# A chunk's scan in whole-chunk instructions, a shorter scale, and counting by a scan and two products

## The chip, the cores and the metric

The kernel runs on one core of one Trainium2 chip. The metric is the device time of one execution in microseconds (us); less is better. A core has TensorE (matrix products), VectorE, ScalarE and GpSimd (elementwise work), and queues of DMA transfers, of which SP's and GpSimd's matter here. Each engine executes its own instructions in their order; semaphores make one engine wait for another or for a transfer.

## The reference

There are 20224 tokens (4 sequences of 5056) with 256 channels each. First, along each sequence and for each channel, a gated recurrence:

```python
sig = 1.0 / (1.0 + np.exp(-f_logit))
f = lower_bound + (1.0 - lower_bound) * sig
for t in range(S):
    h = f[:, t] * h + (1.0 - f[:, t]) * x[:, t]
    y[:, t] = h
```

Then a mixture of eight experts, one for each token:

```python
logits = y @ w_gate                       # 8 columns
e_idx = argmax(logits, axis=1)
gate_w = softmax(logits)[e_idx]
eom = sigmoid(y @ w_output_gate)[e_idx]   # 8 columns
out = gate_w * eom * (relu(y @ w1[e_idx]) @ w2[e_idx])   # 256 -> 1024 -> 256
```

All products are made from pairs of 16-bit numbers, a high part and the low rest (high x high, high x low, low x high), after scaling by powers of two.

## The kernel before

**Chunks.** The inputs lie with channels on the 128 partitions, so a chunk of 512 tokens is two blocks (k = 0, 1) of 128 x 512. There are 40 chunks, the last of 256 tokens. `chunk` (L254) is a generator. A bare `yield` ends a round; `yield SMALL` or `yield BIG` stands ahead of one VectorE instruction. In its rounds a chunk does, in this order: tanh on ScalarE (L265); on VectorE (f - 1) * x, with f still the tanh (L269); on ScalarE the affine map from tanh to the gate f (L274); the recurrence by one scan instruction for each block, cut where a sequence ends (L280); the sum of squares of h on ScalarE (L287) and on TensorE (L291), from which `pow2` (L134) makes a power of two and its inverse in five steps on VectorE. As tanh stands in for the sigmoid, the scan's result still lacks a factor for each channel, `na`; it enters through `na2` at L291 and through `sa` (L296). Then the high half (L310, ScalarE) and the low half (L314, VectorE) of the scaled h, four DMA transposes on SP's queue that bring them into rows, one for each token (L307), and the products with the gates' weights (L329, 16 small matmuls). The result is brought back (L341) with the scale `li`.

**Routing.** Some fifteen small VectorE instructions find each token's expert (`oh`, a one for its expert, L372) and its factor. `before` (L383) counts: a product with a triangle of ones gives how many earlier tokens of a block went to the same expert, and a product with ones for each further block adds the earlier blocks; that is nb + 1 = 5 products for the four blocks of 128 tokens. With the running count `cnt` this gives each token a row `dst` in the scratch `scr` in DRAM, sorted by expert, and GpSimd's queue scatters the rows there (L433).

**Experts.** The weights of all eight experts are prepared once: 16 halves are loaded, normed (`prep_norm`, and `pow2` in `prep_scale`), and split into high (L614, ScalarE) and low (L619, VectorE). Meanwhile `early` (L831) computes two rounds of eight first tiles of 128 tokens, one for each expert: `gather` (L624) brings the tokens' rows from `scr` by a transposing DMA into `xq` and their factors into `mt`, both issued on SP's queue; `first1` makes the first product on TensorE in two halves (h = 0, 1), ScalarE brings it out (L719), `first_low` (L722) makes its low half on VectorE, `first2` the second product. `factors` (L644) multiplies the tokens' factors in `mt` by the expert's, into `fac`, which `evacuate` (L739) uses. From about 184 us on, `experts` (L921) does tiles of 256 tokens: a copy of the expert's first weights (L657, VectorE), `gemm1` (L669 to L671), `gemm2` (L702 to L704).

**Order.** `pump` (L790) takes every live chunk and the tile's tasks one round further; a new chunk begins every 8 rounds, and `load_chunk` for the next one is issued at a chunk's fifth round. Inside a round `together` (L153) puts small instructions of one chunk between those of others. Up to the cut at L907 a planner of the framework is free to reorder the instructions of VectorE, ScalarE, TensorE and GpSimd by its own simulated times; SP's queue and all that stands behind the cut keep the written order (`ordered`, L911). Behind the cut the small matmuls of a chunk are put one by one between an expert's triples of large ones (`aside`, `beside`, L227 and L232).

Of the kernel before, what the change touches and what calls it, by code (L numbers as in the profile page):

```python
# [24 lines left out]
EXPO = 0x7F800000  # L25
TW = 7
TX = 8
# [23 lines left out]
def tile_scan_moe(  # L51
# [66 lines left out]
    cinv = cp.tile([P, E], F32, name="cinv")  # L118

# [6 lines left out]
    na = cp.tile([P, KD], F32, name="na")  # L126
    na2 = cp.tile([P, KD, P], BF16, name="na2")
# [6 lines left out]
    def pow2(ss, t, nm):  # L134
# [5 lines left out]
        iv = sp.tile([P, w], F32, tag=nm + "i", name=nm + "i", bufs=3)  # L140
        yield SMALL
# [4 lines left out]
        nc.vector.tensor_scalar(vi, vi, EXPO, None, ALU.bitwise_and)  # L146
        yield SMALL
        nc.vector.tensor_scalar(sc, v, 2.0 ** (62 + t), None, ALU.mult)
        yield SMALL
        nc.vector.tensor_scalar(iv.bitcast(I32), sc.bitcast(I32), EXPO, None, ALU.bitwise_xor)  # L150
        return sc, iv
# [25 lines left out]
    gsq = cp.tile([P, KD * G], F32, name="gsq")  # L177
# [8 lines left out]
    gi4 = cp.tile([P, 1], F32, name="gi4")  # L186
    nc.vector.tensor_scalar(gi4, giv, 0.25, None, ALU.mult)
# [66 lines left out]
    def chunk(c):  # L254
# [5 lines left out]
        hss = sp.tile([P, KD], BF16, tag="hss", name="hss")  # L260
        cuts = [0] + [q for q in range(1, n) if (t0 + q) % S == 0] + [n]
        f = [ft[:, k, 0:n] for k in range(KD)]
        h = [xt[:, k, 0:n] for k in range(KD)]
        for k in range(KD):
            nc.scalar.activation(f[k], f[k], AF.Tanh, scale=0.5)  # L265
# [19 lines left out]
        with nc.allow_low_precision("a scale's bound"):  # L285
            for k in range(KD):
                nc.scalar.activation(f[k], h[k], AF.Square, accum_out=hss[:, k : k + 1])  # L287
# [6 lines left out]
        sa = sp.tile([P, KD], F32, tag="sa", name="sa")  # L294
        yield SMALL
        nc.vector.tensor_scalar(sa, na, sx, None, ALU.mult)  # L296
        li = sp.tile([P, 1], F32, tag="li", name="li")
        yield SMALL
        nc.vector.tensor_tensor(out=li, in0=ix, in1=gi4, op=ALU.mult)  # L299
# [8 lines left out]

        for k in range(KD):
            nc.scalar.activation(hl[:, 0, k, 0:n], xt[:, k, 0:n], AF.Copy, scale=sa[:, k : k + 1])  # L310
        yield
        for k in range(KD):
            yield BIG
            nc.vector.scalar_tensor_tensor(  # L314
                out=hl[:, 1, k, 0:n], in0=xt[:, k, 0:n], scalar=sa[:, k : k + 1], in1=hl[:, 0, k, 0:n],
                op0=ALU.mult, op1=ALU.subtract,
            )
            turn(0, k)
# [22 lines left out]
        nc.scalar.activation(lgp[:, 0:nb], pr[:, 0:nb], AF.Copy, scale=li)  # L341
# [28 lines left out]
        oh = small("oh", E, BF16)  # L370
# [10 lines left out]
        pk = pp.tile([P, (NB + 1) * E], F32, tag="rw", name="pk")  # L381
        ohf = oh[:, 0:nb].rearrange("p b e -> p (b e)")
        w = nb * E  # L383
        def before(s):
            ww = w if s == 0 else (nb + 1 - s) * E
            nc.tensor.matmul(
                out=pk[:, s * E : s * E + ww], lhsT=ones if s else tri, rhs=ohf[:, 0:ww], start=(s == 0), stop=(s == nb),
                skip_group_check=True,
            )
# [11 lines left out]
        pos = small("pos", E)  # L401
        yield SMALL
        nc.vector.tensor_tensor(
            out=pos[:, 0:nb], in0=pk[:, 0:w].rearrange("p (b e) -> p b e", e=E),
            in1=cnt.unsqueeze(1).to_broadcast([P, nb, E]), op=ALU.add,
        )
        cn = sp.tile([P, E], F32, tag="cnt", name="cnt", bufs=4)
# [599 lines left out]
```

## Time and profile before

| what | value |
|---|---|
| time, median of 3 runs (lowest, highest) | 989.14 us (987.89, 991.45) |
| the profiled execution: its time, its span | 990.77 us, 989.1 us |
| mean granted TensorE clock | 0.988 |
| busy: TensorE matmul, weight load | 907.7 us (92%), 819.7 us (83%) |
| busy: VectorE, ScalarE, GpSimd | 801.0 us (81%), 519.7 us (53%), 390.1 us (39%) |
| instructions of VectorE, ScalarE | 2639, 1075 |
| moved by DMA | 146.56 MB |

The span runs from the first to the last instruction. In a row of the profile L12 is line 12 of the kernel; `out<-in` names the tiles an instruction writes and reads; `x40` is how many there are. A group's row gives busy time and mean duration in ns, then the engine's idle time just ahead of those instructions and what ended it. Weight loads run beside matmuls, and matmuls overlap, so that their durations add up to more than the time they take. A wait is put down to what ended last.

### The profile page before, as it was taken

How to read it: one execution, taken by the hardware profiler on the slowest of the kernel's cores; microseconds unless marked ns; L12 is line 12 of the kernel's file. 1: busy time of each engine (PE TensorE's matmuls, PEld its weight loads, DVE VectorE, ACT ScalarE, POOL GpSimd, SP SyncE). 2: the span in 40 equal slices, each digit the busy share in tenths (PEclk: the TensorE clock that was granted, in tenths of full speed). 3: DMA queues.
4: the chain of work that ended last, by engine and by line, in shares of the span. 5: the costliest groups of instructions: out<-in, count | busy, mean ns of one | idle time of the engine just before them, and what ended most of it. 6: DMA issues, size and time to landing. Idle time of an engine off the chain costs nothing. (4 is left out here: it accounts for less than half of the span.)

```text
span 989.1 us, 30907 instructions
## 1 busy us (share of the span) xinstructions
PE 907.7 (92%) x9775; PEld 819.7 (83%) x9775; DVE 801.0 (81%) x2639; ACT 519.7 (53%) x1075; POOL 390.1 (39%) x378
## 2 busy tenths in 40 slices
PE   2258898899999999999999999999999999999993
PEld 2247887788888888888888888888888888899992
DVE  7989897888989988888898888888888886545550
ACT  6667675555555555555565555555555543333331
POOL 1432334434445454454545434455444443211111
PEclk9999999999999999999999999999999999999997
DMA  8899984855575657556576665655666544312120
GB/s 310 206 275 293 237 230 126 188 157 151 131 157 144 151 153 167 141 133 152 150 153 150 169 138 140 153 148 157 150 163 134 129 100 90 100 45 43 41 57 17
DMA packets 238558, 146.56 MB, mean 148 GB/s; under 512 B 202557, under 2 KB 204223, under 8 KB 238400
## 3 DMA queue, kind: packets, MB, share of 16 engines
q1 hardware_dynamic: 222752, 101.74, 44.9%
q0 software_dynamic: 15360, 42.74, 14.4%
q8 instruction: 95, 1.56, 0.7%
q14 instruction: 63, 0.52, 0.2%
q10 hardware_dynamic: 288, 0.02, 0.0%
HBM read 58.38 MB, written 44.49 MB: 104 GB/s over the span
## 5 line engine op out<-in xcount | busy, mean ns | idle before, releaser
L674 ACT ACTIVATE hh<-ph 128x512 f16<-128x512 f32 (+1 forms) x328 | 180.4, 550 | 307.8 <-PE ph L671 297.4
L669 PE MATMUL ph<-xq,w 128*128 128x256 f16 (+1 forms) x1312 | 330.4, 260 | 2.9 <-DMA xq<-scr 2.4
L671 PE MATMUL ph<-xq,w 128*128 128x256 f16 (+1 forms) x1312 | 331.1, 261 | 0.0
L670 PE MATMUL ph<-xq,w 128*128 128x256 f16 (+1 forms) x1312 | 330.9, 261 | 0.0
L750 POOL DMA_INDIRECT out_dram<-yo,mt x146 | 175.3, 1201 | 363.2 <-ACT yo L746 339.9
L704 PE MATMUL py<-w2s,hl 128*128 x1168 | 318.5, 273 | 0.0
L703 PE MATMUL py<-w2s,hh 128*128 x1168 | 318.4, 273 | 0.0
L702 PE MATMUL py<-w2s,hh 128*128 x1168 | 318.1, 272 | 0.0
L682 DVE SCALAR_TENSOR_TENSOR hl<-ph,hh 128x512 f16<-128x512 f32 (+1 forms) x328 | 204.9, 625 | 58.2 <-ACT hh L674 55.8
L433 POOL DMA_INDIRECT scr<-rows,dst x154 | 175.7, 1141 | 122.6 <-issue 109.3
L657 DVE COPY w<-w1s 128x2048 f16 x164 | 120.3, 734 | 35.1 <-PE ph L671 33.3
L669 PEld LDWEIGHTS <-w 128*128 128x128 f16 x1312 | 127.9, 98 | 14.3 <-DVE fac L649 2.7
L671 PEld LDWEIGHTS <-w 128*128 128x128 f16 x1312 | 128.0, 98 | 11.9
L670 PEld LDWEIGHTS <-w 128*128 128x128 f16 x1312 | 127.9, 97 | 9.7
L704 PEld LDWEIGHTS <-hl 128*128 128x128 f16 x1168 | 114.1, 98 | 13.8
L702 PEld LDWEIGHTS <-hh 128*128 128x128 f16 x1168 | 114.0, 98 | 11.4
L703 PEld LDWEIGHTS <-hh 128*128 128x128 f16 x1168 | 113.9, 98 | 10.6
L280 DVE TENSOR_TENSOR_SCAN xt<-ft,xt 128x512 f32<-128x512 f32 (+4 forms) x78 | 90.8, 1172 | 0.0
L746 ACT ACTIVATE yo<-py,fac 128x256 f32<-128x256 f32 x146 | 61.8, 468 | 26.7 <-PE py L704 26.1
L314 DVE SCALAR_TENSOR_TENSOR ft<-xt,sa,ft 128x512 f16<-128x512 f32 (+1 forms) x76 | 56.2, 744 | 20.1 <-ACT ft L265 18.3
L329 PEld LDWEIGHTS <-ft 128*128 128x128 f16 x600 | 51.7, 99 | 15.1 <-ACT ft L310 4.9
L310 ACT ACTIVATE ft<-xt,sa 128x512 f16<-128x512 f32 (+1 forms) x76 | 50.2, 707 | 23.3 <-DVE li L299 16.0
(171 smaller groups left out, 1298.7 us busy)
## 6 DMA issues: line engine op xcount, KB each, us to landing
ft<-in_fT_dram SPq DMA_DIRECT2D x37, 512.0 KB
xt<-in_xT_dram SPq DMA_DIRECT2D x37, 512.0 KB
w<-in_wT_dram SPq DMA_DIRECT2D x32, 512.0 KB
scr<-rows,dst POOLq DMA_INDIRECT x154
rows<-ft SPq DMA_TRANSPOSE x152
out_dram<-yo,mt POOLq DMA_INDIRECT x146
xq<-scr SPq DMA_TRANSPOSE x99
scr<-padt SPq DMA_DIRECT2D x9, 136.0 KB
```

The source lines that it names most:

```text
L280: nc.vector.tensor_tensor_scan(out=xt[:, k, a:z], data0=ft[:, k, a:z], data1=xt[:, k, a:z], initial=init, op0=ALU.mult, op1=ALU.add)
L433: ins = nc.gpsimd.indirect_dma_start(out=scr[:, :], out_offset=IOA(ap=dst[:, b : b + 1], axis=0), in_=rows[:, b, :], in_offset=None)
L657: nc.vector.tensor_copy(out=w, in_=w1f[:, ds(T["ev"] * (2 * WH) + h * 2 * QH, 2 * QH)])
L669: nc.tensor.matmul(out=o, lhsT=w[:, f, k, 0, :], rhs=T["xh"][:, k, 0:n], start=first, stop=False)
L670: nc.tensor.matmul(out=o, lhsT=w[:, f, k, 0, :], rhs=T["xl"][:, k, 0:n], start=False, stop=False)
L671: nc.tensor.matmul(out=o, lhsT=w[:, f, k, 1, :], rhs=T["xh"][:, k, 0:n], start=False, stop=last)
L674: nc.scalar.activation(hh[:, :, 0:n], ph[:, :, 0:n], AF.Relu)
L682: nc.vector.scalar_tensor_tensor(out=hl[:, :, 0:n], in0=ph[:, :, 0:n], scalar=0.0, in1=hh[:, :, 0:n], op0=ALU.max, op1=ALU.subtract)
L702: nc.tensor.matmul(out=o, lhsT=hh[:, i, c], rhs=wh, start=first, stop=False, skip_group_check=True)
L703: nc.tensor.matmul(out=o, lhsT=hh[:, i, c], rhs=wl, start=False, stop=False, skip_group_check=True)
L704: nc.tensor.matmul(out=o, lhsT=hl[:, i, c], rhs=wh, start=False, stop=last, skip_group_check=True)
L750: ins = nc.gpsimd.indirect_dma_start(out=out[:, :], out_offset=IOA(ap=T["mt"][:, b, 2:4].bitcast(I32), axis=0), in_=T["yo"][:, b, :], in_o ...
```

## The change

- Tanh is one instruction for the whole chunk (two blocks), then come the two affine maps, and the product on VectorE uses the finished gate: (f - 1) * x. The scan so gives -h in full, and the factors `na`, `na2` and `sa` go; the power of two is made negative instead.
- The squares, the high half and the low half are one instruction each for the whole chunk; the sum of squares has one column and one product with ones.
- `pow2` has four steps in place of five, for chunks and for weights.
- `li` goes: the gates' results are brought back with the chunk's inverse alone, and the gates' own scale `gi4` enters as the scale of the two exponentials.
- The ones of the experts go into one of two fixed tiles with a column of zeros ahead of the blocks (`ones_of`). A scan of 40 elements on VectorE (`upto`), which begins anew at each expert, sums the earlier blocks; one product with ones and one with the triangle then give all counts, the total in a fifth column, and the running count is added in one instruction instead of two.
- `factors` of a first tile is done with its second half's low part, not with the first's.
- Small tiles are set once at the start (`going`, `ones_of`: four memsets on GpSimd).

```diff
+    going = cp.tile([P, E * (NB + 1)], BF16, name="going")
+    nc.gpsimd.memset(going, 1.0)
+    nc.gpsimd.memset(going.rearrange("p (e b) -> p e b", e=E)[:, :, 0:1], 0.0)
+    ones_of = [cp.tile([P, E, NB + 1], BF16, name=f"onesof{i}") for i in range(2)]
+    for t in ones_of:
+        nc.gpsimd.memset(t, 0.0)
-    nc.vector.tensor_scalar(na, lbt, 0.5, -0.5, ALU.mult, ALU.add)
-    for k in range(KD):
-        nc.vector.tensor_scalar(na2[:, k, :], ones, na[:, k : k + 1], na[:, k : k + 1], ALU.mult, ALU.mult)
...
-        nc.vector.tensor_scalar(vi, vi, EXPO, 1, ALU.bitwise_xor, ALU.logical_shift_right)
-        nc.vector.tensor_scalar(vi, vi, EXPO, None, ALU.bitwise_and)
-        nc.vector.tensor_scalar(sc, v, 2.0 ** (62 + t), None, ALU.mult)
-        nc.vector.tensor_scalar(iv.bitcast(I32), sc.bitcast(I32), EXPO, None, ALU.bitwise_xor)
+        nc.vector.tensor_scalar(vi, vi, EVEN, 1, ALU.bitwise_and, ALU.logical_shift_right)
+        nc.vector.tensor_scalar(sc.bitcast(I32), vi, -1.0, float(top - (1 << 31 if minus else 0)), ALU.mult, ALU.add)
+        nc.vector.tensor_scalar(iv.bitcast(I32), vi, float(EXPO - top), None, ALU.add)
...
+        nc.scalar.activation(fb2, fb2, AF.Tanh, scale=0.5)
+        yield
         for k in range(KD):
-            nc.scalar.activation(f[k], f[k], AF.Tanh, scale=0.5)
-        yield
+            nc.scalar.activation(f[k], f[k], AF.Identity, scale=fa[:, k : k + 1], bias=fb[:, k : k + 1])
+        yield
         for k in range(KD):
             yield BIG
             nc.vector.scalar_tensor_tensor(
-                out=h[k], in0=f[k], scalar=1.0, in1=h[k], op0=ALU.subtract, op1=ALU.mult
+                out=xt[:, k, 0:n], in0=f[k], scalar=1.0, in1=xt[:, k, 0:n], op0=ALU.subtract, op1=ALU.mult
             )
-        yield
-        for k in range(KD):
-            nc.scalar.activation(f[k], f[k], AF.Identity, scale=fa[:, k : k + 1], bias=fb[:, k : k + 1])
...
-            for k in range(KD):
-                nc.scalar.activation(f[k], h[k], AF.Square, accum_out=hss[:, k : k + 1])
+            nc.scalar.activation(fb2, hb2, AF.Square, accum_out=hss)
-        for k in range(KD):
-            nc.tensor.matmul(out=pv, lhsT=na2[:, k, :], rhs=hss[:, k : k + 1], start=(k == 0), stop=(k == KD - 1))
-        yield
-        sx, ix = yield from pow2(pv, TX, "x")
-        nc.vector.tensor_scalar(sa, na, sx, None, ALU.mult)
-        nc.vector.tensor_tensor(out=li, in0=ix, in1=gi4, op=ALU.mult)
+        nc.tensor.matmul(out=pv, lhsT=ones, rhs=hss, start=True, stop=True)
+        yield
+        sx, ix = yield from pow2(pv, TX, "x", minus=True)
...
+        nc.scalar.activation(hl[:, 0, :, 0:n], hb2, AF.Copy, scale=sx)
+        yield
+        yield BIG
+        nc.vector.scalar_tensor_tensor(
+            out=hl[:, 1, :, 0:n], in0=hb2, scalar=sx, in1=hl[:, 0, :, 0:n], op0=ALU.mult, op1=ALU.subtract
+        )
...
+        upto = sp.tile([P, E * (NB + 1)], BF16, tag="upto", name="upto")
+        yield SMALL
+        nc.vector.tensor_tensor_scan(
+            out=upto, data0=going, data1=ohz.rearrange("p e b -> p (e b)"), initial=0.0, op0=ALU.mult, op1=ALU.add
+        )
...
-            ww = w if s == 0 else (nb + 1 - s) * E
-            nc.tensor.matmul(
-                out=pk[:, s * E : s * E + ww], lhsT=ones if s else tri, rhs=ohf[:, 0:ww], start=(s == 0), stop=(s == nb),
-                skip_group_check=True,
-            )
-        for s in range(nb + 1):
+            if s == 0:
+                o = pk.rearrange("p e b -> p (e b)")
+                nc.tensor.matmul(out=o, lhsT=ones, rhs=upto, start=True, stop=False, skip_group_check=True)
+            else:
+                nc.tensor.matmul(
+                    out=pk[:, :, 0:NB], lhsT=tri, rhs=ohz[:, :, 1:], start=False, stop=True, skip_group_check=True
+                )
+        for s in range(2):
             aside(before, s)
...
-        nc.scalar.activation(ex[:, 0:nb], dl[:, 0:nb], AF.Exp)
+        nc.scalar.activation(ex[:, 0:nb], dl[:, 0:nb], AF.Exp, scale=gi4[:, 0:1])
-        nc.scalar.activation(eg[:, 0:nb], gs[:, 0:nb], AF.Exp, scale=-1.0)
+        nc.scalar.activation(eg[:, 0:nb], gs[:, 0:nb], AF.Exp, scale=gi4[:, 1:2])
...
         for T, h in wait:
             tasks.append(first_low(T, h))
-            if h == 0:
+            if h == 1:
                 tasks.append(factors(T))
```

More of the change, by code (lines that the diff above doesn't have):

```diff
@@ L25 @@
 EXPO = 0x7F800000
+EVEN = 0x7F000000
 TW = 7
@@ L125, in tile_scan_moe, with pow2 @@
     fb = cp.tile([P, KD], F32, name="fb")
-    na = cp.tile([P, KD], F32, name="na")
-    na2 = cp.tile([P, KD, P], BF16, name="na2")
     nc.vector.tensor_scalar(fa, lbt, -0.5, 0.5, ALU.mult, ALU.add)
     nc.vector.tensor_scalar(fb, lbt, 0.5, 0.5, ALU.mult, ALU.add)
-    nc.vector.tensor_scalar(na, lbt, 0.5, -0.5, ALU.mult, ALU.add)
-    for k in range(KD):
-        nc.vector.tensor_scalar(na2[:, k, :], ones, na[:, k : k + 1], na[:, k : k + 1], ALU.mult, ALU.mult)
-    def pow2(ss, t, nm):
+    def pow2(ss, t, nm, minus=False):
         w = ss.shape[1]
@@ L140, in pow2 @@
         iv = sp.tile([P, w], F32, tag=nm + "i", name=nm + "i", bufs=3)
+        top = EVEN // 2 + ((62 + t) << 23)
         yield SMALL
@@ L174, in alone @@
                 return end.value
-    gsq = cp.tile([P, KD * G], F32, name="gsq")
+    gsq = sp.tile([P, NB, 2 * G], F32, tag="lgp", name="gsq").rearrange("p b g -> p (b g)")[:, 0 : KD * G]
     gss = cp.tile([P, 1], BF16, name="gss")
@@ L185, in tile_scan_moe @@
     gsc, giv = alone(pow2(pgs, TW, "gt"))
-    gi4 = cp.tile([P, 1], F32, name="gi4")
-    nc.vector.tensor_scalar(gi4, giv, 0.25, None, ALU.mult)
+    gi4 = cp.tile([P, 2], F32, name="gi4")
+    nc.vector.tensor_scalar(gi4[:, 0:1], giv, 0.25, None, ALU.mult)
+    nc.vector.tensor_scalar(gi4[:, 1:2], giv, -0.25, None, ALU.mult)
     wgs = cp.tile([P, KD, 2, G], F16, name="wgs")
@@ L259, in chunk @@
         xt, ft = loaded.pop(c)
-        hss = sp.tile([P, KD], BF16, tag="hss", name="hss")
+        hss = sp.tile([P, 1], BF16, tag="hss", name="hss")
         cuts = [0] + [q for q in range(1, n) if (t0 + q) % S == 0] + [n]
+        fb2, hb2 = ft[:, :, 0:n], xt[:, :, 0:n]
         f = [ft[:, k, 0:n] for k in range(KD)]
-        h = [xt[:, k, 0:n] for k in range(KD)]
+        nc.scalar.activation(fb2, fb2, AF.Tanh, scale=0.5)
+        yield
         for k in range(KD):
-            nc.scalar.activation(f[k], f[k], AF.Tanh, scale=0.5)
+            nc.scalar.activation(f[k], f[k], AF.Identity, scale=fa[:, k : k + 1], bias=fb[:, k : k + 1])
         yield
@@ L307, in turn @@
             nc.sync.dma_start_transpose(out=rows[:, 0:nb, q * P : (q + 1) * P], in_=hl[:, i, k, 0:n].bitcast(I16))
-        for k in range(KD):
-            nc.scalar.activation(hl[:, 0, k, 0:n], xt[:, k, 0:n], AF.Copy, scale=sa[:, k : k + 1])
-        yield
[L312 to L316, printed above, removed]
-            )
+        nc.scalar.activation(hl[:, 0, :, 0:n], hb2, AF.Copy, scale=sx)
[4 more added lines that the diff above has]
+        )
+        for k in range(KD):
             turn(0, k)
@@ L340, in chunk @@
         lgp = sp.tile([P, NB, 2 * G], F32, tag="lgp", name="lgp")
-        nc.scalar.activation(lgp[:, 0:nb], pr[:, 0:nb], AF.Copy, scale=li)
+        nc.scalar.activation(lgp[:, 0:nb], pr[:, 0:nb], AF.Copy, scale=ix)
         yield
@@ L369, in chunk @@
         nc.vector.tensor_reduce(out=km[:, 0:nb], in_=key[:, 0:nb], axis=AX.X, op=ALU.max)
-        oh = small("oh", E, BF16)
+        ohz = ones_of[c % 2]
+        oh = ohz[:, :, 1:].rearrange("p e b -> p b e")
         yield SMALL
@@ L400, in chunk @@
         cnt = state["cnt"]
-        pos = small("pos", E)
+        pos = sp.tile([P, NB + 1, E], F32, tag="cnt", name="cnt", bufs=4)
         yield SMALL
         nc.vector.tensor_tensor(
-            out=pos[:, 0:nb], in0=pk[:, 0:w].rearrange("p (b e) -> p b e", e=E),
-            in1=cnt.unsqueeze(1).to_broadcast([P, nb, E]), op=ALU.add,
-        )
-        cn = sp.tile([P, E], F32, tag="cnt", name="cnt", bufs=4)
+            out=pos[:, 0 : nb + 1], in0=pk.rearrange("p e b -> p b e")[:, 0 : nb + 1],
+            in1=cnt.unsqueeze(1).to_broadcast([P, nb + 1, E]), op=ALU.add,
+        )
+        state["cnt"] = cn = pos[:, nb, :]
+        own = small("own", E)
         yield SMALL
-        nc.vector.tensor_tensor(out=cn, in0=cnt, in1=pk[:, w : w + E], op=ALU.add)
-        state["cnt"] = cn
-        yield SMALL
-        nc.vector.tensor_tensor(out=pos[:, 0:nb], in0=pos[:, 0:nb], in1=oh[:, 0:nb], op=ALU.mult)
+        nc.vector.tensor_tensor(out=own[:, 0:nb], in0=pos[:, 0:nb], in1=oh[:, 0:nb], op=ALU.mult)
         dst = small("dst", None, I32)
@@ L415, in chunk @@
         with nc.allow_low_precision("whole numbers"):
-            nc.vector.tensor_reduce(out=dst[:, 0:nb], in_=pos[:, 0:nb], axis=AX.X, op=ALU.add)
+            nc.vector.tensor_reduce(out=dst[:, 0:nb], in_=own[:, 0:nb], axis=AX.X, op=ALU.add)
         es = small("es")
```

10 lines of the change are left out of this document (1 added, 9 removed).

## The prediction

> **What bounds the kernel now.** First the busy times of seven stretches (columns: TensorE matmul, weight load, VectorE, ScalarE, GpSimd, granted TensorE clock, DMA share, GB/s).
>
> ```profile
> 0.00:60.00 60.00, 14.47 (x179) 11.45 (x180) 50.31 (x199) 38.67 (x74) 16.96 (x35) 1.00 0.92 260
> 60.00:100.00 40.00, 31.23 (x415) 28.93 (x414) 34.95 (x115) 26.03 (x43) 11.37 (x12) 1.00 1.10 286
> 100.00:150.00 50.00, 46.52 (x674) 44.03 (x675) 43.80 (x142) 36.88 (x65) 16.93 (x17) 0.97 0.90 232
> 150.00:205.00 55.00, 47.80 (x555) 42.43 (x553) 43.95 (x151) 28.67 (x63) 21.17 (x21) 0.94 0.63 156
> 205.00:835.00 630.00, 630.00 (x6280) 565.04 (x6279) 553.84 (x1848) 340.96 (x721) 293.95 (x264) 1.00 0.61 145
> 835.00:972.00 137.00, 137.00 (x1676) 127.52 (x1675) 74.10 (x189) 48.06 (x113) 28.75 (x29) 1.00 0.23 57
> ```
>
> From 205 to 972 us TensorE is busy for every microsecond: 767 of 989 us go at the pace of its instruction stream, and VectorE's 554 us in there lie beside it. A busy matmul is not yet a matmul at its peak, so next the timeline of TensorE alone (start, duration; matmuls overlap, so starts are what counts).
>
> ```profile
> 400.15 0.27 PE L671 MATMUL ph<-xq,w 128*128 128x256 f16 x1
> 400.26 0.17 PE L386 MATMUL pk<-oh,ones 128*128 128x16 bf16 x1
> 400.29 0.27 PE L702 MATMUL py<-w2s,hh 128*128 x1
> ...
> 401.62 0.27 PE L669 MATMUL ph<-xq,w 128*128 128x256 f16 x1
> ...
> 402.93 0.27 PE L702 MATMUL py<-w2s,hh 128*128 x1
> ```
>
> Twelve 256-column matmuls start in 402.93 - 401.62 = 1.31 us, 0.109 each. The count L386 takes 400.29 - 400.26 = 0.03. So here a chunk's small matmul costs about 0.03 us, not its shown 0.17.
>
> Before 205 us TensorE waits. The waits of TensorE from 60 to 205 us, longest first (total, times, longest):
>
> ```profile
> PE ph L715 <- DMA xq<-scr: 12.8, 6, 3.7
> PE py L737 <- DVE el L726: 2.8, 4, 1.9
> PE ph L669 <- DMA xq<-scr: 2.4, 1, 2.4
> ```
>
> The end is therefore: the fill up to 60 us, some 20 us of stalls up to 205, and TensorE's work. Only an edit that touches one of the three moves the end.
>
> **The change, part by part.** (1) Fewer matmuls. Per chunk, counting goes from five products to two and the scale's sum from two to one. How many of L386, then L291, then L329 (the gates) lie in the three stretches:
>
> ```profile
> 0.00:60.00 60.00, 1.15 (x20) 0.96 (x20) 1.00 0.92 260
> 60.00:205.00 145.00, 2.17 (x30) 1.93 (x30) 0.96 0.85 218
> 205.00:835.00 630.00, 25.82 (x148) 14.30 (x148) 1.00 0.61 145
> ...
> 205.00:835.00 630.00, 5.35 (x56) 5.48 (x56) 1.00 0.61 145
> ...
> 205.00:835.00 630.00, 45.74 (x456) 44.24 (x456) 1.00 0.61 145
> ```
>
> In the full stretch 148 x 3/5 + 56 / 2 = 117 matmuls go. Their price from the stretch itself: 148 + 56 + 456 = 660 of the 6280 are small, the other 5620 x 0.109 take 613 us, and 17 us / 660 is 0.026 us. The pair above says 0.03. 117 x 0.026 to 0.03 is 3.0 to 3.5 us; I take **3.3 us**. Nothing covers it: there is no gap beside it. The 40-column product has no row; columns cost 0.109/256 each, so 24 more are at most 0.01 us, 0.3 us in all, and I keep it in the 3.0.
>
> The Trainium skill ("Trainium Kernel Development and Optimization", section Performance Expectations) has weight-load busy time as the good measure of distance to the roofline, not matmul busy time. L386's 148 loads took 14.30 us, 0.097 each, so by loads the 117 would give 11.3 us, and the time would be 974 us in place of the sum below. The pair of starts 0.03 us apart, shorter than one such load, speaks against it; the row decides.
>
> (2) VectorE. These rows give the mean of one instruction in ns, after the busy time:
>
> ```profile
> L314 DVE SCALAR_TENSOR_TENSOR ft<-xt,sa,ft 128x512 f16<-128x512 f32 (+1 forms) x76 | 56.2, 744 | 20.1 <-ACT ft L265 18.3 <-DMA xq<-scr 0.6 <-ACT hh L674 0.6
> L619 DVE SCALAR_TENSOR_TENSOR w1s<-w,ws,w1s 128x1024 f16<-128x1024 f32 x16 | 20.4, 1279 | 0.1
> L296 DVE TENSOR_SCALAR sa<-na,xs 128x2 f32<-128x2 f32 x40 | 9.1, 228 | 0.0
> L299 DVE TENSOR_TENSOR li<-xi,gi 128x1 f32<-128x1 f32 x40 | 6.8, 169 | 0.0
> L148 DVE TENSOR_SCALAR xs<-xv 128x1 f32<-128x1 f32 x40 | 6.1, 152 | 1.1
> L409 DVE TENSOR_TENSOR cnt<-cnt,pk 128x8 f32<-128x8 f32 x39 | 5.9, 151 | 0.0
> L500 DVE TENSOR_TENSOR_SCAN pl_cum<-one,pl_av 128x8 f32<-128x8 f32 x33 | 5.8, 175 | 1.1
> L280 DVE TENSOR_TENSOR_SCAN xt<-ft,xt 128x512 f32<-128x512 f32 (+4 forms) x78 | 90.8, 1172 | 0.0
> ```
>
> The low half of a chunk in one instruction of 1024 has its like in L619: 2 x 0.744 - 1.279 = 0.21 us less. Gone are one step of the scale (0.15), sa (0.23), li (0.17) and the separate count (0.15). New is a scan of 40, between the scans of 8 and 512: 0.175 + 32 x 0.997/504 = 0.24. Sum: **0.67 us less per chunk**. Small instructions overlap on VectorE, so the lower end is 0.45. By 205 us ten chunks have been counted (20 + 30 matmuls at five each), and the 16 weight halves lose one scale step each: 10 x 0.67 + 16 x 0.15 = 9.1 us less VectorE work (6.9 at the lower end), 3.3 of it before 60 us (four chunks, and a quarter of the halves taken as done by then). After 205 us this is hidden behind full TensorE and worth nothing; if TensorE were not full, it would be 30 x 0.67 = 20 us, which is not claimed.
>
> (3) ScalarE. Tanh, square and high half become one instruction each, of 1024:
>
> ```profile
> L310 ACT ACTIVATE ft<-xt,sa 128x512 f16<-128x512 f32 (+1 forms) x76 | 50.2, 707 | 23.3 <-DVE li L299 16.0 <-DVE sa L296 6.0 <-DVE pos L403 1.3
> L287 ACT ACTIVATE ft<-xt 128x512 f32<-128x512 f32 (+1 forms) x76 | 46.5, 616 | 10.4 <-DVE xt L280 5.6 <-DVE wv L146 1.9 <-issue 1.6
> L265 ACT ACTIVATE ft<-ft 128x512 f32<-128x512 f32 (+1 forms) x76 | 43.0, 615 | 11.4 <-DMA ft<-in_fT_dram 8.0 <-issue 3.4
> L614 ACT ACTIVATE w1s<-w,ws 128x1024 f16<-128x1024 f32 x16 | 17.4, 1138 | 3.7 <-DVE ws L148 2.0 <-DMA out_dram<-ey,mt 1.7
> L287 ACT ACTIVATION_READ_ACCUMULATOR ft<-xt 128x1 bf16 x76 | 14.7, 193 | 0.0
> ```
>
> High half: 2 x 0.707 - 1.138 = 0.28 less (the row of 1024 is a Copy with a scale too). Each extra element costs (1.138 - 0.707)/512, so tanh and square of 1024 are 1.05 each and save 0.18 each, and one read of the accumulator saves 0.19: 0.8 us per chunk. The two exponentials now take their scale from a tile; the difference of 0.707 and 0.615 bounds that by 0.09 each. Against it, the first half of a chunk reaches VectorE later: tanh by 0.43 us, high half by 0.43. With 130 of 205 us busy (38.67 + 26.03 + 36.88 + 28.67) ScalarE is not the bound, so I count nothing for either by itself.
>
> (4) Order inside a chunk: Identity now follows tanh on ScalarE and the product with x comes after both. One hand-over between engines goes, the number of rounds stays, and the loads, the transposes on SP's queue and the scatters on GpSimd's are issued in the same rounds.
>
> (5) The factors of the first tiles move one round later. The waits of VectorE from 60 to 205 us, and the longest stall's place:
>
> ```profile
> DVE fac L649 <- DMA mt<-scr: 8.5, 7, 3.8
> DVE el L726 <- ACT eh L719: 3.3, 4, 1.3
> ...
> 165.58 0.21 DVE L649 TENSOR_SCALAR fac<-mt,cinv 128x1 f32<-128x1 f32 x1 [3.79 <-DMA mt<-scr]
> ...
> 167.25 0.68 DVE L726 SCALAR_TENSOR_TENSOR el<-ph,eh 128x512 f16<-128x512 f32 x1
> ```
>
> Up to 8.5 us of VectorE waiting goes. But the first half's low part, L726, comes in the same round and needs xq, which was issued just ahead of mt: it starts at 167.25, 1.7 us after the factors. What is late next is L726, so most of the stall moves there. TensorE's wait is for xq and not for the factors. Bounds 0 to 8.5 us of VectorE time; I count 1 us on the path.
>
> (6) Set-up: four GpSimd memsets are added, VectorE loses L130 and two L132. SP's first issue waits for the pad, the loads stand behind it:
>
> ```profile
> 2.95 0.10 POOL L443 MEMSET done<- 128x8 f32 x1
> 3.00 0.14 POOL L210 IOTA padt<- 128x1 int32 x1
> ...
> 3.16 0.38 SPq L211 DMA_DIRECT2D scr<-padt  x1
> ```
>
> Four memsets of 0.10 us ahead of the pad make all loads 0.4 us late, behind it 0. I take 0.2.
>
> **The sum.** Fill to 60 us: VectorE is busy 50.31 of 60 and TensorE waits on the chunks' chain; of 3.3 us I put 2 on the path, less 0.2. From 60 to 205: of 5.8 us (9.1 - 3.3) about a third, 2 us, since 100 to 150 us is nearly full on TensorE, plus the 1 us of (5), less 0.8 that I hold back for a planner that lays this stretch out anew. Early **4.0 us** (bounds: 0 and 9.1 + 8.5 = 17.6 gained; a loss is the third rival). With 3.3 it is 7.3 us. The profiled execution took 990.77 us (span 989.1): 983.5. It lies 1.63 above the median of 989.14, so the median after is 981.8; forecast **982 us**.
>
> **The rivals.** *TensorE alone.* The early stalls are for xq, a DMA that follows a scatter; VectorE's gain goes into waiting for it. Also the case where whole-chunk instructions give nothing. Against it: 84% busy VectorE up to 60 us. Early 0 to 1.5: 984.4 to 985.8.
>
> *The clock.* Three stretches of TensorE run at half clock (0.50 in the third column from the end; the first and the last of three, a third at 166 to 169 us):
>
> ```profile
> 101.20:104.60 3.40, 3.40 (x40) 3.40 (x38) 2.77 (x10) 1.80 (x5) 2.10 (x2) 0.50 1.08 368
> ...
> 193.40:196.80 3.40, 3.40 (x29) 2.52 (x25) 3.40 (x6) 1.52 (x3) 1.75 (x3) 0.50 0.71 168
> ```
>
> Each costs half of 3.4, 1.7 us. If shorter stalls for xq avoid all three, 5.1 us come on top of the forecast: 977. Each follows a stall that DMA ends, which the change shortens only indirectly. The Trainium skill ("TensorE: Matmul & The Clock Gate", section What's actually happening) halves the clock after an idle window of about 3.4 us whose phase is free-running; the granted-clock rows agree in length, and by that rule a new gap could as well add 1.7 us.
>
> *Slower: first tiles queue behind whole-chunk instructions.* Before the cut the planner chooses the order, and first tiles' L719 and L726 share ScalarE and VectorE with chunks. Each chunk has one longer VectorE instruction (by 1.279 - 0.744 = 0.54) and three longer on ScalarE (0.43 each): at worst 1.8 us per chunk if every one stands ahead of a tile's instruction that TensorE waits for. Ten chunks: 18 us, less 3.3 and the early 4: 1000 us. It decides from 7.3 us, four chunks in ten. For it: L737 already waits 2.8 us for L726. Against: only four such waits now, in 32 halves. Half of the worst case gives 991 us.
>
> **Chances.** Forecast (979 to 984) 0.52; TensorE alone (984 to 987) 0.22; the clock or VectorE's whole gain (below 979) 0.14; slower 0.12 (987 and up, mostly above 989). The range of 8 in 10 reaches down into the clock's case and up to where the slower rival begins: 975 to 989.5. 0.3% is 3 us, about what a measurement can tell here. Faster by more (below 986.2): 0.52 + 0.14 + half of 0.22 = 0.77, less 0.02 for a rest unseen. Within: 0.15. Slower (above 992.1): 0.10.
>
> **What would show it.** TensorE without a gap after the first expert tile, and its 2 + 1 small matmuls per chunk about 0.026 us apart: (1). A whole-chunk low half near 1.28 us and high half near 1.14, the scan near 0.24: (2), (3). The first L669 of the experts some 4 us earlier: the early sum. No wait of the factors for mt, and a longer one of L726 for L719: (5). The first load on SP 0.2 us later: (6). Wrong, if the first L669 isn't earlier, or if gaps show after 205 us.

## The result, and the profile after

The changed kernel takes 1004.12 us (median; 1002.30 to 1005.71) against 989.41 us for the kernel before (987.89 to 991.45): a ratio of **1.0147 [1.0118, 1.0175]**. It is slower by about 15 us, where 982 was forecast. The profiled execution took 1005.46 us, its span is 1003.8.

First the page after, span and busy times:

```profile
span 1003.8 us, 30118 instructions
...
PE 908.7 (91%) x9617; PEld 818.1 (81%) x9617; DVE 787.2 (78%) x2460; ACT 511.8 (51%) x915; POOL 412.8 (41%) x382
```

789 instructions fewer, 158 of them matmuls, and yet a longer span. Where the time went is in the same stretches that the prediction read (columns as there: TensorE matmul, weight load, VectorE, ScalarE, GpSimd, granted TensorE clock, DMA share, GB/s):

```profile
0.00:60.00 60.00, 12.27 (x162) 10.14 (x163) 47.19 (x167) 33.83 (x49) 20.92 (x40) 0.73 0.81 237
60.00:100.00 40.00, 29.07 (x379) 26.73 (x379) 32.45 (x99) 25.63 (x37) 10.36 (x12) 0.81 1.04 277
100.00:150.00 50.00, 43.84 (x576) 40.69 (x575) 39.56 (x115) 31.36 (x47) 16.82 (x13) 0.90 1.00 229
150.00:205.00 55.00, 41.52 (x516) 36.45 (x515) 35.25 (x118) 25.32 (x45) 19.87 (x20) 0.91 0.51 123
205.00:835.00 630.00, 629.65 (x6179) 563.40 (x6178) 547.87 (x1730) 342.26 (x615) 311.12 (x264) 1.00 0.63 149
```

After 205 us TensorE is as full as before (629.65 of 630). Before 205 us it was busy for 14.47 + 31.23 + 46.52 + 47.80 = 140.0 us in the old kernel and is busy for 12.27 + 29.07 + 43.84 + 41.52 = 126.7 us in the new one; it has started 1633 matmuls by then against 1823, of which some 40 are products that the change takes away (four for each of ten chunks). So it reaches the experts late. The start of the experts is the first product of line L669, L668 in the new text. Rows of that line between 170 and 215 us (count, shortest, median and longest duration in ns, first and last start); before, then after:

```profile
L669 PE MATMUL ph<-xq,w x48: 269/272/374, 184.5 to 214.0; 128*128 128x256 f16 x48
```

```profile
L668 PE MATMUL ph<-xq,w x23: 269/273/417, 202.3 to 214.8; 128*128 128x256 f16 x23
```

That product was to come 4 us earlier, and it comes 17.8 us later. It is the whole loss: 17.8 us late at the start of the experts, some 3 us given back in the full stretch, 14.7 in the spans.

What TensorE waits for from 60 to 205 us (total, times, longest), to be held against the three rows in the prediction:

```profile
PE ph L714 <- DMA xq<-scr: 18.0, 7, 8.9
PE ph L668 <- DMA xq<-scr: 6.7, 1, 6.7
PE py L734 <- ACT eh L718: 4.4, 2, 2.6
PE py L736 <- DVE el L725: 1.9, 2, 1.7
```

The waits for gathered rows (xq) grow from 12.8 + 2.4 to 18.0 + 6.7 us, and a wait for ScalarE's eh of 4.4 us is new. The same view for VectorE:

```profile
DVE fac L648 <- DMA mt<-scr: 14.4, 8, 3.6
DVE xt L275 <- ACT ft L270: 5.2, 2, 4.6
DVE cnt L404 <- PE pk L388: 5.0, 1, 5.0
DVE w2s L618 <- ACT w2s L613: 4.1, 2, 3.8
DVE jk L584 <- PE pg L577: 2.9, 2, 1.6
```

VectorE has less to do and waits more: for mt 14.4 us in place of 8.5, and 5.2 us at the product with x (L275), which now stands behind Identity (L270). This looks like a pipeline that is out of step rather than an engine that is overloaded; the experiments test it. The clock may add to it; four stretches of the new kernel at about half clock:

```profile
27.00:71.40 44.40, 10.78 (x142) 9.41 (x142) 37.62 (x141) 26.60 (x42) 21.13 (x19) 0.50 0.85 216
88.40:91.80 3.40, 3.40 (x29) 2.74 (x27) 3.40 (x5) 0.66 (x2) 0.00 (x0) 0.55 1.07 368
105.50:112.30 6.80, 5.12 (x49) 5.12 (x50) 3.23 (x13) 5.36 (x8) 4.36 (x4) 0.52 0.99 307
197.60:207.80 10.20, 5.50 (x28) 3.94 (x29) 3.14 (x15) 1.75 (x3) 1.24 (x2) 0.52 0.62 153
```

TensorE is busy for 24.8 us in them, so at most half of that, 12 us, is the clock's; the three stretches of the kernel before cost 5.1. But the execution with the lowest clock isn't the slowest: the four executions of the new kernel took 1005.46, 1002.79, 1005.71 and 1002.30 us at mean clocks of 0.957, 0.983, 0.984 and 0.963. And the same kernel on another chip (the run "as it is" under "The order tied") went through the longest of the four stretches at full clock, with TensorE just as sparsely busy:

```profile
27.00:71.40 44.40, 10.51 (x152) 9.15 (x152) 37.57 (x142) 27.09 (x42) 20.96 (x19) 1.00 0.85 216
```

Its experts started at 199.6 us all the same. So most of the lateness is there without that stretch of half clock.

### The profile page after: what moved, and what is told of

Its sections match the earlier page's. It is cut to its first block, busy times and chain, and to the rows that moved or that the text cites. A ratio compares the mean times of both kernels' runs of the same rounds, so it can differ in the third digit from the quotient of the medians.

```text
span 1003.8 us, 30118 instructions
## 1 busy us (share of the span) xinstructions
PE 908.7 (91%) x9617; PEld 818.1 (81%) x9617; DVE 787.2 (78%) x2460; ACT 511.8 (51%) x915; POOL 412.8 (41%) x382
## 4 chain that ended last, share of the span: by engine, by line
PE 69%; issue 11%; DMA 6%; DVE 4%; POOL 2%; SPq 2%; ACT 1%; POOLq 0%; DVEq 0%; ACTq 0%
PE ph L668 11%; PE py L701 11%; PE ph L670 11%; PE ph L669 11%; PE py L702 11%; PE py L703 11%; DMA xq<-scr 3%; POOL out_dram L749 2%; DMA ft<-in_fT_dram 1%; DVE xt L283 1%; PE pr L322 1%; DMA rows<-ft 1%; SPq L302 1%; DVE el L725 1%; DVE w2s L618 1%
## 5 line engine op out<-in xcount | busy, mean ns | idle before, releaser
L668 PE MATMUL ph<-xq,w 128*128 128x256 f16 (+1 forms) x1312 | 331.6, 261 | 7.0 <-DMA xq<-scr 7.0
L669 PE MATMUL ph<-xq,w 128*128 128x256 f16 (+1 forms) x1312 | 331.9, 261 | 0.0
L749 POOL DMA_INDIRECT out_dram<-yo,mt x146 | 187.5, 1284 | 350.8 <-ACT yo L745 328.8
L681 DVE SCALAR_TENSOR_TENSOR hl<-ph,hh 128x512 f16<-128x512 f32 (+1 forms) x328 | 204.8, 624 | 52.2 <-ACT hh L673 49.6
L432 POOL DMA_INDIRECT scr<-rows,dst x154 | 180.5, 1172 | 119.8 <-issue 109.0
L668 PEld LDWEIGHTS <-w 128*128 128x128 f16 x1312 | 128.4, 98 | 14.8 <-DVE xv L145 2.5
L669 PEld LDWEIGHTS <-w 128*128 128x128 f16 x1312 | 128.2, 98 | 14.7 <-issue 4.3
L307 DVE SCALAR_TENSOR_TENSOR ft<-xt,xs,ft 128x1024 f16<-128x1024 f32 (+1 forms) x38 | 48.3, 1270 | 22.2 <-ACT hh L673 20.1
L714 PE MATMUL ph<-xq,w1s 128*128 128x128 f16 x256 | 49.3, 231 | 18.0 <-DMA xq<-scr 18.0
```

What stands on the lines that cost most here:

```text
L432: ins = nc.gpsimd.indirect_dma_start(out=scr[:, :], out_offset=IOA(ap=dst[:, b : b + 1], axis=0), in_=rows[:, b, :], in_offset=None)
L668: nc.tensor.matmul(out=o, lhsT=w[:, f, k, 0, :], rhs=T["xh"][:, k, 0:n], start=first, stop=False)
L669: nc.tensor.matmul(out=o, lhsT=w[:, f, k, 0, :], rhs=T["xl"][:, k, 0:n], start=False, stop=False)
L681: nc.vector.scalar_tensor_tensor(out=hl[:, :, 0:n], in0=ph[:, :, 0:n], scalar=0.0, in1=hh[:, :, 0:n], op0=ALU.max, op1=ALU.subtract)
L749: ins = nc.gpsimd.indirect_dma_start(out=out[:, :], out_offset=IOA(ap=T["mt"][:, b, 2:4].bitcast(I32), axis=0), in_=T["yo"][:, b, :], in_o ...
```

## The experiments

Each ratio is to the kernel before on the same chip. On three of the chips (the first twelve kernels below, up to the order tied on three engines or fewer) the kernel before takes 1006 to 1007 us instead of 989 to 990; what differs there is told at the end. As that difference lies mostly behind the start of the experts, their ratios hold more than the early stretch, and the start of the experts is given beside them where it says more. With the four memsets of the null edit, which stands for the kernel before there, it is 187.8 us.

### Parts of the change undone

**Written order.** In both kernels the planner may not reorder the early stretch.

```diff
-    ordered(0, prog["cut"])
+    ordered(0, 0)
```

> The kernel before, with the written order kept on every engine from the start: the planner may not move VectorE's, ScalarE's, TensorE's and GpSimd's instructions up to the cut. It is the reference for the next run. Theory P (the planner laid the early stretch of the changed kernel out worse, the change's own work is not slower): some time above 989 us, 990 to 1030, and the next run 3 to 9 us below this one. Theory M (whole-chunk instructions hold up the first tiles on VectorE and ScalarE) and theory F (the factors one round later): nothing about this run by itself, but the next run 10 to 18 us above it.

> The changed kernel, with the written order kept on every engine from the start. Theory P: 3 to 9 us below the run before it (TensorE's 4 us of work, and some of VectorE's 9 us). Theories M and F: 10 to 18 us above the run before it, as with the planner (1004 against 989).

Measured: the kernel before in its written order 1.0176 [1.0095, 1.0257], the changed one 1.0197 [1.0091, 1.0304]. Two executions of each (1020.82 and 1026.11 us, and 1021.67 and 1029.57) tell no difference between them: neither the 3 to 9 us less of theory P nor the 10 to 18 us more of M and F shows. In the written order the kernel before loses all that it was ahead, which points to something that the planner had made of it.

**Factors back.** The changed kernel with the factors at their old step.

```diff
-            if h == 1:
+            if h == 0:
                 tasks.append(factors(T))
```

> The changed kernel with the first tiles' factors done with the first half's low part again, as before. Theory F (the factors' new place makes the early stretch 15 us longer): 984 to 990 us. Theory M: 1002 to 1006, as the changed kernel. Theory P: any value from 984 to 1010, since each edit has the planner lay the stretch out anew.

Measured 1.0108 [1.0035, 1.0182], not the return to 984 to 990 us of theory F. VectorE's wait for mt falls to 7.6 us, yet the experts start at 204.0 us, and the interval overlaps that of the whole change.

**Blocks back.** Tanh, square, high and low half by blocks of 512 again.

```diff
-        nc.scalar.activation(fb2, fb2, AF.Tanh, scale=0.5)
+        for k in range(KD):
+            nc.scalar.activation(f[k], f[k], AF.Tanh, scale=0.5)
...
-        nc.scalar.activation(hl[:, 0, :, 0:n], hb2, AF.Copy, scale=sx)
...
         for k in range(KD):
+            nc.scalar.activation(hl[:, 0, k, 0:n], xt[:, k, 0:n], AF.Copy, scale=sx)
```

> The changed kernel with tanh, squares, high half and low half done by blocks of 512 again, two instructions each; all else as changed. Theory M (longer instructions ahead of the first tiles' own): 984 to 990 us. Theory F: 1002 to 1006. Theory P: any value from 984 to 1010.

Measured 1.0175 [1.0122, 1.0227]: no gain, and theory M missed. The planner laid this kernel out anew too, so this alone doesn't clear the length of whole-chunk instructions, the prediction's slower rival; a pair with the order tied, further down, does.

The expectations from here to the null edit weigh three theories. C: the new counting costs. M2: the order and the length of a chunk's scan instructions cost. L: any edit that has the planner lay the early stretch out anew loses about 1%.

**Old counting.** The changed kernel with five products, and no scan and no fixed tiles.

```diff
-                nc.tensor.matmul(out=o, lhsT=ones, rhs=upto, start=True, stop=False, skip_group_check=True)
...
-        for s in range(2):
+        for s in range(nb + 1):
             aside(before, s)
```

> The changed kernel with the old counting by five products, without the scan of 40 and without the four memsets. Theory C: from 0.7% below the kernel before to 0.3% above it. Theory M2: 1.0 to 1.8% above. Theory L: 0.5 to 2% above.

Measured 1.0103 [1.0051, 1.0156]. Again no return to 1, so the counting alone isn't it (theory C). The experts start at 196.0 us.

### Parts of the change alone

**Four steps alone.** The kernel before with only the new power of two.

```diff
-        nc.vector.tensor_scalar(vi, vi, EXPO, 1, ALU.bitwise_xor, ALU.logical_shift_right)
-        nc.vector.tensor_scalar(vi, vi, EXPO, None, ALU.bitwise_and)
+        nc.vector.tensor_scalar(vi, vi, EVEN, 1, ALU.bitwise_and, ALU.logical_shift_right)
...
```

> The kernel before with the scale in four steps instead of five, no other edit: strictly one VectorE instruction less for each chunk and each half of the weights. Theory L: 0.5 to 1.5% above the kernel before. Theories M2 and C: 0 to 0.4% below it.

Measured 1.0101 [1.0065, 1.0137]. Here only work was taken away, one short VectorE instruction for each scale, and the kernel is 1% slower, with the experts at 203.1 us. That is theory L, and from here on the order itself was the suspect.

**Swap and whole-chunk instructions alone** (Identity ahead of the product, no `na`, one instruction per chunk; one small VectorE instruction makes the scale's sign).

```diff
+        nc.scalar.activation(fb2, fb2, AF.Tanh, scale=0.5)
+        yield
         for k in range(KD):
-            nc.scalar.activation(f[k], f[k], AF.Tanh, scale=0.5)
+            nc.scalar.activation(f[k], f[k], AF.Identity, scale=fa[:, k : k + 1], bias=fb[:, k : k + 1])
...
-        for k in range(KD):
-            nc.scalar.activation(f[k], f[k], AF.Identity, scale=fa[:, k : k + 1], bias=fb[:, k : k + 1])
...
```

> The kernel before with the changed scan: Identity ahead of the product with x, the factor for each channel gone, tanh, squares, high and low half in whole-chunk instructions; the scale keeps its five steps, one small VectorE instruction makes its sign, and the counting, the gates' scale and the factors are as before. Theory M2: 1.0 to 1.8% above the kernel before, as the whole change. Theory C: from 0.5% below to 0.3% above it. Theory L: 0.5 to 1.5% above.

Measured 1.0446 [1.0399, 1.0493], more than any theory foretold. About a third of these 45 us comes in the early stretch as in the others (experts at 202.7 us, 14.9 later than with the null edit); the rest is a loss behind it that no other kernel has to this extent, told of at the end.

**Four memsets alone**, as a null edit.

```diff
+    for i in range(4):
+        nc.gpsimd.memset(cinv, float(i))
```

> The kernel before with four tiny GpSimd memsets added at the start, of a tile that is written later anyway; no other edit. Theory L (the constants of the kernel before were fitted to one order of the early stretch, and any edit that has the planner lay it out anew loses 1% or so): 0.5 to 1.5% above the kernel before. Theories M2 (order and length of a chunk's scan instructions) and C (the new counting): within 0.4% of it.

Measured 1.0016 [0.9991, 1.0041], under the 0.5 to 1.5% of theory L. In the profiles of this kernel and the kernel before, VectorE, ScalarE and TensorE execute the same sequence up to the start of the experts: an edit that leaves the order as it was costs nothing that can be told. So theory L holds at most for edits that do change the order.

### The order tied

In the following kernels the instructions of the early stretch are tied on an engine, each behind the one ahead of it, in a given order:

```diff
+                for a, b in zip(names[:-1], names[1:]):
+                    tc.add_manual_dep(held[b], a, AFTER, reason="order")
```

First the changed kernel itself on another chip, and then with the factors at their old step and the order of the kernel before on three engines, on VectorE alone, and on ScalarE and GpSimd alone. TensorE was left to the planner.

> The changed kernel again, on the chip of the next three. Every theory: 1.2 to 1.8% above the kernel before on the same chip.

> The changed kernel (its factors at the first half's place, which by itself moved nothing in the early stretch), with VectorE's, ScalarE's and GpSimd's instructions of the early stretch put in the order that the planner had given the kernel before: each instruction at the place of the one it stands for, a merged one at the place of one of its two (tanh, high and low half at the first, squares at the second), Identity straight behind tanh, the scan behind the ones it sums. Theory P (the planner's new order is the loss): 0.3 to 0.9% below the kernel before, 981 to 986 where before is 989, so that the prediction's sum stands. Theory M (the new instructions themselves hold up the first tiles): 0.8 to 1.8% above it, with the order of before too.

> As the run before, but only VectorE's order is the old one; ScalarE's and GpSimd's are the planner's own. Theory P, if VectorE's order is what counts: within 0.5% of the run before. If ScalarE's is: within 0.5% of the changed kernel. Theory M: as the changed kernel.

> As two runs before, but only ScalarE's and GpSimd's order is the old one; VectorE's is the planner's own. Theory P, if VectorE's order is what counts: within 0.5% of the changed kernel. If ScalarE's is: within 0.5% of the run in the old order on all engines. Theory M: as the changed kernel.

Measured: 1.0166 [1.0122, 1.0210] as it is; 1.0152 [1.0099, 1.0204], 1.0192 [1.0143, 1.0241] and 1.0187 [1.0100, 1.0275] tied. None of them helps (experts at 199.6 us as it is, and at 198.7, 204.3 and 204.8 tied), and theory P's 0.3 to 0.9% below the kernel before didn't come. But this doesn't clear the order: TensorE was loose in all of them, and merged instructions don't have one old place.

So the question was put where no instruction has to be merged, with all four engines tied. **One set of instructions, two orders**: the four-step kernel in the order of the kernel before, and the kernel before, unchanged, in the order that the planner had given to the four-step kernel. And the kernel before with nothing but the factors written one step later (`h == 0` to `h == 1`).

> The kernel with only the four-step powers of two (ratio 1.010 when planned afresh), its VectorE, ScalarE, GpSimd and TensorE instructions of the early stretch now tied in the order that they have in the kernel before. Theory O (the order that the planner lays out anew is what costs): ratio 0.997 to 1.002, experts start within 2 us of the kernel before. Rival W (the four-step instructions themselves, or their waits, cost): the ratio stays at 1.007 to 1.014, experts start 12 us or more later.

> The kernel before, no instruction changed, its early stretch tied in the order that the planner gave the kernel with only the four-step powers of two (each extra step right behind the one ahead of it). Theory O: ratio 1.006 to 1.015, experts start 10 us or more later, with the same work. Rival W: ratio within 0.998 to 1.003.

> The kernel before with only the first tiles' factors one step later: no instruction changes, only where the code writes them. Theory O: the planner lays the early stretch out anew, so 1.004 to 1.02. Rival (only work and the wait for the table count): within 0.997 to 1.003, since the planner puts the factors where their inputs allow.

Measured: **1.0000 [0.9986, 1.0014]**, **1.0102 [1.0081, 1.0122]** and **1.0041 [1.0023, 1.0059]**. The first two settle it for the four-step power: its whole loss of 1% goes with the order and comes with the order (experts at 187.0 and 195.1 us, 184.5 in the kernel before), and the instructions themselves count for nothing that can be told. The third settles little: its interval touches both forecasts, and the experts start 1.1 us later (185.6). Of the stretches before 205 us, the last two, first of the four-step kernel in the old order:

```profile
100.00:150.00 50.00, 44.73 (x649) 41.73 (x647) 42.39 (x134) 35.80 (x60) 18.35 (x17) 0.97 0.97 221
150.00:205.00 55.00, 47.22 (x572) 42.70 (x570) 44.61 (x145) 29.94 (x63) 21.18 (x21) 0.97 0.71 151
```

and of the kernel before in the four-step kernel's order:

```profile
100.00:150.00 50.00, 45.61 (x647) 42.43 (x645) 42.23 (x129) 32.87 (x58) 18.04 (x17) 0.97 0.87 226
150.00:205.00 55.00, 41.48 (x514) 36.28 (x515) 38.64 (x137) 27.05 (x56) 18.67 (x19) 0.94 0.58 143
```

In the latter TensorE, VectorE, ScalarE and GpSimd are all less busy from 150 to 205 us: 41.48 against 47.22, 38.64 against 44.61, and so on. Each of the four waits more. The granted clock hardly differs, so the order costs its 10 us without the clock. What waits differs from order to order; TensorE's waits from 60 to 205 us in the latter:

```profile
PE ph L677 <- DMA xq<-scr: 6.5, 2, 5.2
PE ph L723 <- DMA xq<-scr: 5.3, 4, 2.9
PE py L745 <- DVE el L734: 5.0, 6, 1.8
PE py L745 <- DVE wv L152: 4.1, 2, 2.2
```

Here the waits for rows are shorter than before (11.8 us in place of 15.2) and those for VectorE are longer. No single wait stands out as the one to remove.

**The changed kernel in the old order on all four engines**, with the factors at their old step, then the same with blocks of 512 again (edits as above).

> The changed kernel (factors at their old step), with the instructions of the early stretch tied on all four engines, TensorE too, in the order of the kernel before: a merged instruction stands where the first of its parts stood, the two counting products where the last two of the five stood. Theory O alone (any order but the old one costs): 0.994 to 1.000, as the order comes back and the 4 us of TensorE work stay saved. Rival J (the old order suits only the old instructions: a whole-chunk instruction hands over later than the first of two halves, so the old order stalls behind it): 1.006 to 1.017, the lag beginning in chunk 0, where the high half ends 2 us later.

> The changed kernel in the order of the kernel before on all four engines, as in the run just above, but with tanh, square, high and low half by blocks of 512 again, each in its old place; Identity ahead of the product, four-step scales, negative scale and counting by a scan and two products stay. Theory J (the longer whole-chunk instructions are what no longer fits the old order): 0.995 to 1.000, the high half of chunk 0 ends within 0.5 us of the kernel before. Rival S (Identity ahead of the product, or the scan of the count, is what doesn't fit): 1.004 to 1.010.

Measured 1.0075 [1.0052, 1.0098] and 1.0077 [1.0048, 1.0106]. Theory O alone (0.994 to 1.000) missed: about half of the loss of the changed kernel goes with the order on four engines, the place of the factors included, which these runs don't separate; the other half stays. As the second is no faster than the first, the length of the whole-chunk instructions is not what holds that half (theory J missed; the second came within the 1.004 to 1.010 of rival S). The experts start at 197.4 and 191.7 us in the two profiles, the first of which took the slowest of its six executions. One thing that stays is to be seen on ScalarE early on. The kernel before:

```profile
17.64 1.13 ACT L265 ACTIVATE ft<-ft 128x512 f32<-128x512 f32 x2
18.68 1.32 ACT L310 ACTIVATE w2s<-w2s,sa 128x512 f16<-128x512 f32 x2
19.91 1.32 ACT L310 ACTIVATE ft<-xt,sa 128x512 f16<-128x512 f32 x2
21.13 1.50 ACT L274 ACTIVATE ft<-ft,fb,fa 128x512 f32<-128x512 f32 x2
```

and the changed one by blocks, tied:

```profile
17.67 1.13 ACT L276 ACTIVATE ft<-ft 128x512 f32<-128x512 f32 x2
18.71 1.50 ACT L279 ACTIVATE ft<-ft,fb,fa 128x512 f32<-128x512 f32 x2
20.12 1.32 ACT L316 ACTIVATE w2s<-w2s,xs 128x512 f16<-128x512 f32 x2
21.34 1.32 ACT L316 ACTIVATE ft<-xt,xs 128x512 f16<-128x512 f32 x2
```

Identity (L274, now L279) has to come ahead of the product with x, so I placed it right behind tanh, and there chunk 2's Identity stands ahead of chunk 0's high half, which starts 1.44 us later (20.12 against 18.68). Little of it arrives: VectorE's low half of chunk 0 starts only 0.64 us later (20.86 against 20.22), and the gates' result is brought back 0.41 us later (22.95 against 22.54). That such delays repeat and make up the rest is possible and not shown: the swap wasn't run alone in a tied order, and the scan of the count may have its share.

### The change in the late stretch only

The kernel before up to chunk 11, so that the early stretch is the same instruction for instruction; from chunk 12 on the changed chunk, except that `li` and the plain exponentials stay. The weights' scale and the place of the factors are those of the kernel before.

```diff
-        for kind in chunk(c):
+        for kind in chunk(c) if c < TURNED else chunk_late(c):
```

> The kernel before up to chunk 11, so the whole early stretch is instruction for instruction the same; from chunk 12 on the changed scan, whole-chunk instructions, four-step power and counting by two products. Step 1 of the prediction (110 fewer small products at 0.026 to 0.03 us in the stretch where TensorE never stalls): 2.9 to 3.3 us less, ratio 0.996 to 0.998, experts start as before. If the change costs in the late stretch too (TensorE waits there on these chips): 1.000 or more.

Measured 985.79 us against 989.85, **0.9963 [0.9947, 0.9979]**: faster than both kernels. Its page, its experts' first product and its full stretch:

```profile
span 986.4 us, 30387 instructions
...
PE 906.7 (92%) x9665; PEld 818.7 (83%) x9665; DVE 791.6 (80%) x2556; ACT 510.6 (52%) x963; POOL 404.2 (41%) x382
```

```profile
L881 PE MATMUL ph<-xq,w x48: 269/272/374, 184.7 to 214.1; 128*128 128x256 f16 x48
```

```profile
205.00:835.00 630.00, 630.00 (x6196) 564.97 (x6194) 546.45 (x1769) 332.85 (x610) 309.31 (x265) 1.00 0.62 146
```

The experts start at 184.7 us (184.5 before), TensorE is full, and it has 9775 - 9665 = 110 matmuls fewer. The spans differ by 989.1 - 986.4 = 2.7 us, 0.025 us each; the ratio says 3.7 us [2.1, 5.2]. VectorE has 630 - 546 us to spare there, so the gain is put down to the matmuls. For a chunk this is the change as it was meant, without its price.

## Why the prediction was wrong

**The bound** was read rightly: fill, early stalls, TensorE's stream. Nearly all that changed lies in the second and third.

**(1) Fewer matmuls, 3.3 us: right.** 110 of them gave 2.7 us between the two profiles and 3.7 [2.1, 5.2] by the ratio, with 0.026 to 0.03 each foretold. The rule that the prediction weighed here, the Trainium skill ("Trainium Kernel Development and Optimization", section Performance Expectations) with weight-load busy time as a good measure of the distance to the roofline, would make it 110 x 0.097 = 10.7 us, an estimate. The runs decide against taking it as a price for these small products.

**(2) and (3) Durations: right one by one.** The new rows:

```profile
L307 DVE SCALAR_TENSOR_TENSOR ft<-xt,xs,ft 128x1024 f16<-128x1024 f32 x37 | 47.5, 1284 | 21.6 <-ACT hh L673 19.4 <-DVE rows L429 1.3 <-ACT ft L304 0.7
L377 DVE TENSOR_TENSOR_SCAN upto<-going,onesof 128x40 bf16<-128x40 bf16 x40 | 9.3, 231 | 0.0
L304 ACT ACTIVATE ft<-xt,xs 128x1024 f16<-128x1024 f32 x37 | 42.4, 1147 | 13.7 <-DVE xi L152 12.2 <-DVE xs L150 1.2 <-DVE ws L150 0.4
L289 ACT ACTIVATE ft<-xt 128x1024 f32<-128x1024 f32 x37 | 38.9, 1051 | 16.6 <-issue 9.6 <-DVE xt L283 5.5 <-ACT lgp L334 0.8
```

Low half 1.284 us (1.279 foretold), scan 0.231 (0.24), high half 1.147 (1.138), square 1.051 (1.05). VectorE's total fell by 801.0 - 787.2 = 13.8 us, under the 20 that the lower end made of it; but the unchanged instructions of the kernel before read 799.0 in the four-step kernel's order and 795.0 with the factors written later, so the total isn't good to better than some us.

**(4) The order inside a chunk, counted as nothing: open, and not nothing in the one place seen.** "One hand-over goes" overlooked that 1.5 us of Identity moves ahead of VectorE's product; at chunk 0 of the tied kernel it holds up the high half by 1.44 us and the low half behind it by 0.64, and 5.2 us of VectorE's waits stand at that product in the changed one.

**(5) The factors one step later, 1 us gained: wrong in sign.** The wait for mt didn't go, it grew to 14.4 us; in the kernel before with this edit alone it grew to 13.3, and the whole time by 0.4%. The planner is free to place the factors; writing them later didn't put them where their input had come.

**(6) Set-up, 0.2 us: right.** SP's first issue is 0.22 us later (columns: start, duration):

```profile
3.38 0.39 SPq L214 DMA_DIRECT2D scr<-padt  x1
```

**The sum is the step that failed: "Early 4.0 us" gained, with bounds of 0 and 17.6.** The early stretch lost 17.8 us, and the prediction's own sign of being wrong came: the first product of the experts isn't earlier. The sum was made as if the order of the instructions stayed and each became shorter. The prediction held back 0.8 us "for a planner that lays this stretch out anew", and that term is the mis-sized one: a new order alone, with not one instruction changed, cost 10 us in the kernel before, and in the changed kernel about half of the loss went when the old order was tied. All that the four-step power takes away was worth 0.0% [-0.14, 0.14] with the order kept. The bound "0 gained" left a loss to the third rival alone, with no reason why a new layout couldn't cost more than 0.8 us.

**The rivals.** The third had the sign and, with 991 to 1000 us, came nearest to 1004.12, but by the wrong mechanism: blocks of 512 helped neither with the order tied nor with the planner free. So its nearness is luck. *TensorE alone* is what the change does where the early stretch is left alone (985.79 measured, 984.4 to 985.8 foretold; by its own terms the lower end is 984.3). The clock moved against the kernel in the profiled execution. By the Trainium skill ("TensorE: Matmul & The Clock Gate", section What's actually happening) the clock is halved after an idle window of about 3.4 us and full again after a busy one, and the phase of the windows is free-running. The trace agrees in the length: the 44.4 us from 27.0 on are 13 such windows. But sparse work need not bring it: on another chip the same stretch ran at full clock, with TensorE busy for 10.51 us in place of 10.78. The tied orders show a loss of 10 us without it.

**Open** stays half of the changed kernel's loss, 0.75%, which goes neither with the old order tied on four engines nor with the length of the instructions.

## What to carry to other kernels

Where several in-order engines feed one another and nobody is full, time can hang on the order of the instructions, and an edit that only shortens work cost 1% here because it was laid out anew: price the new layout with a range on both sides. Tell work from order by running one set of instructions in two orders, on all engines at once; tying three of the four or fewer told nothing here. And an edit that pays in the full stretch can be kept out of the early one, as the last experiment did.

## What was not expected of the hardware

The same kernel took 989 us on some chips and 1006 on others. On the latter TensorE has short gaps in the full stretch that nothing in the profile ends. Here is the kernel with the four memsets from 215 to 835 us, its stretch and its longest waits of TensorE (total, times, longest):

```profile
215.00:835.00 620.00, 612.63 (x6065) 544.88 (x6063) 532.18 (x1774) 325.91 (x703) 253.13 (x256) 1.00 0.62 145
```

```profile
PE pr L331 <- issue: 3.7, 9, 0.6
PE py L704 <- issue: 1.3, 3, 0.7
```

7.4 us are missing there, where the kernel before showed 630.00 of 630. The kernel with the swap and whole-chunk instructions alone shows far more of them, 23.5 us:

```profile
215.00:835.00 620.00, 596.47 (x5745) 520.56 (x5744) 506.19 (x1679) 306.12 (x564) 250.47 (x240) 0.99 0.60 140
```

Why some chips have these gaps, and why that kernel has the most, none of the runs tells.

One small price, which the prediction had only bounded by 0.09 us, came out at that bound: an exponential whose scale comes from a tile takes 0.31 us (changed kernel, first row) where the plain one took 0.22 (kernel before).

```profile
L395 ACT ACTIVATE ex<-dl,gi 128x32 f32<-128x32 f32 x39 | 12.0, 311 | 0.7 <-DVE dl L353 0.7
```

```profile
L394 ACT ACTIVATE ex<-dl 128x32 f32<-128x32 f32 x39 | 8.6, 221 | 1.7 <-DVE dl L360 1.7
```
